# Taking the last output products of a group in one-pass forms, behind the group's last hidden block

## The chip, the cores and the metric

One core of one Trainium2 chip. The metric is the device time of one execution in microseconds (us). TensorE does matrix products into PSUM, ScalarE (ACT) and VectorE (DVE) do elementwise work and empty PSUM, SyncE's queue (SP) issues nearly all DMAs.

## The reference

Two blocks, one after the other. The first is a linear attention with RMS normalisation per head; the second a two-layer network with the activation h * erf(softplus(h)). All data are fp32 (the two weight matrices arrive as 64-bit floats).

```python
kv = np.einsum('bhsd,bhse->bhde', k, v)            # batch 8, heads 8, seq 576, head_dim 64
out = np.einsum('bhsd,bhde->bhse', q, kv)
rms = np.sqrt(np.mean(out * out, axis=-1, keepdims=True) + 1e-06)
out = out / rms * g_norm
x = out.transpose(0, 2, 1, 3).reshape(4608, 512)
h = x @ w_in                                       # w_in 512 x 2048
sp = np.maximum(h, 0.0) + np.log1p(np.exp(-np.abs(h)))
g = h * erf(sp)
out = g @ w_out                                    # w_out 2048 x 512
```

## The kernel before, in words

**Tiling.** The 4608 tokens are nine groups T of 512. Groups 0 to 7 are the first 512 tokens of each batch entry; the 64 left over from each entry make group 8. x is held transposed, as 4 blocks (one for each pair of heads, p = 0 to 3) of 128 features by 512 tokens. The 2048 hidden features are 16 blocks f of 128. One pair (T, f) is a *unit*. Its hidden product is 4 matmuls (h block = 128 features by 512 tokens), and its part of the output is 4 matmuls, one for each 128 tokens (column j), each adding 128 x 512 to a bank of PSUM.

**Two kinds of products.** A plain fp32 matmul is two instructions. In the other kind both factors are split into three forms (`upper`, `lower`: high, low, and both, a combination in which the low part is scaled by SHIFT = 4096). Products of high and low forms go to a bank n_ps, products of the third forms to a bank m_ps, and the result is n_ps * (SHIFT - 1) + m_ps. So three one-pass matmuls of type fp32r stand for one fp32 matmul. `product` (L581) writes such a group: eight matmuls into n_ps, then four into m_ps. The split of an operand is one ScalarE operation (high) and two VectorE operations (low, both).

**First stage, the loop at L893**, n = 0 to 32, n = T*16 + f, for groups 0 and 1. The weights lie in the chip's memory in fp32: `w_in_sb` and `w_out_sb`, one tile each, in the pool `first_w`. Group 0 and the first two units of group 1 use plain fp32. From f = 2 of group 1 on, hidden products are in forms (`hidden`, L634), with weights split on the way: `to_cut` says which weight block is split in which step, `w_upper` (L603) does the ScalarE part, `w_lower` (L619) the VectorE part one step later, and each split block is stored to DRAM for the later groups. A split goes into a buffer of the ring `w_in_p`, or, for the steps in `places_w`, into three slots of `w_in_sb` that are no longer needed (a *place*). Each unit is then: hidden product, n_ps emptied by ScalarE and m_ps added by VectorE (`add`, L567), softplus on ScalarE, later erf on ScalarE (a batch of four shares a table load), then the gate h * s on VectorE (`gates`, L886), and five steps (LAG) after the hidden product the four output products in plain fp32 (`project`, L644). In group 1 n_ps and m_ps take the same two banks (pool `ps_h`) in every unit. Units 28 to 31, the last four of group 1, don't go through `project`: their h block is kept (`old_h`) and their output products are taken in forms in the next stage. After unit 27's project the four sums are copied out of PSUM (`sums`, L673) by ScalarE and VectorE in turn.

**Attention in between.** The x of the next group is prepared during the loop, pair by pair, as pieces placed by `pieces_of` (L841): products (`visit`), the square's halves (`halve`), the mean (four small matmuls, then a table load, Ln, Exp, Square on ScalarE), `norm` (three VectorE operations, then a transpose for the next pair), `split` (one ScalarE and two VectorE operations into `x_forms`). For group 2 pair 3, the last, the mean comes at n = 30 and norm and split at n = 31.

**Second stage, from L1000.** Gates of units 28 to 31, then the pools of the first stage are closed, and the ring `w_out_p`, the tiles for `g_forms` and others are opened in that room. The loop at L1048 goes over batches m of four units: four hidden products in forms, then the output products of the batch before (`result`, L1023), with split weights loaded from DRAM (`load_parts`, L829). `load_parts("out", BATCH)` at L1046 issues the first four loads, for the output products of units 28 to 31, before the loop.

**Order.** Every engine works off its instructions in the order in which the program writes them (manual schedule); waits between engines are put in from the data that tiles share, reuse of a tile's room included.

Of the kernel before, what the change touches and what calls it, by code (L numbers as in the profile page):

```python
# [39 lines left out]
FP32 = mybir.dt.float32  # L40
# [10 lines left out]
BATCH = 4  # L51
# [18 lines left out]
def kernel(  # L70
# [106 lines left out]
    for i in range(NP):  # L177
        load_pair(i)

    w_in_sb = first_w.tile([P, FC, KC, P], FP32, name="w_in_sb")  # L180
    w_out_sb = first_w.tile([P, FC, DM], FP32, name="w_out_sb")


    g_col = const.tile([P, 1], FP32, name="g_col")
# [69 lines left out]
    def w_join(which, f, k):  # L254


        scaled, _, hi = words(which, f)
        e, m, late_ = w_cv.pop((which, f))
        w_raw.pop((which, f))
        if late_:  # L260
            nc.vector.tensor_scalar(
                out=e.bitcast(FP32), in0=scaled, scalar1=2.0**-112, scalar2=None, op0=ALU.mult
            )
        nc.vector.tensor_scalar(
            out=e, in0=e, scalar1=3, scalar2=None, op0=ALU.logical_shift_left
        )
        nc.vector.scalar_tensor_tensor(  # L267
            out=e, in0=hi, scalar=-(1 << 31), in1=e, op0=ALU.bitwise_and, op1=ALU.bitwise_or
        )
        if which == "in":  # L270
            out_ = w_in_sb[:, f : f + k].rearrange("p t c f -> p (t c f)")
        else:
            out_ = w_out_sb[:, f : f + k, :].rearrange("p t f -> p (t f)")
        nc.vector.tensor_tensor(out=out_.bitcast(I32), in0=e, in1=m, op=ALU.add)  # L274


# [269 lines left out]
    def thirds(x, high, low, both):  # L546
        upper(x, high)
        lower(x, high, low, both)

    def upper_w(x, high):  # L550
        nc.scalar.activation(high, x, AF.Copy, scale=(1.0 + 2.0**-13) / SHIFT)
# [46 lines left out]
                    )  # L598
        return n_ps, m_ps

    w_kept, w_new, w_now = {}, {}, {}

    def w_upper(which, f, place=None):  # L603


        if place is None:
            t = w_in_p.tile([P, 3, G], FP32R, name="w_new", tag="w")
            parts = t.rearrange("p i (c f) -> p i c f", c=KC)
        else:
            t = None  # L610
            parts = w_in_sb.bitcast(FP32R)[:, 3 * place : 3 * (place + 1)]
        if which == "in":
            x = w_in_sb[:, f]
        else:
            x = w_out_sb[:, f, :].rearrange("p (c f) -> p c f", c=KC)
        upper_w(x, parts[:, 0])
        w_new[which, f] = t, x, parts

    def w_lower(which, f):  # L619

        t, x, parts = w_new.pop((which, f))
        lower_w(x, *(parts[:, i] for i in range(3)))
        kept = w_kept[which, f] = dram.tile([P, 3, G], FP32, name=f"w_{which}{f}")
        for i in range(3):
            if t is None:
                nc.sync.dma_start(
                    out=kept[:, i].rearrange("p (c f) -> p c f", c=KC), in_=parts[:, i].bitcast(FP32)
                )
        if t is not None:
            nc.sync.dma_start(out=kept, in_=t.bitcast(FP32))  # L630
            if which == "in" and f >= WHOLE:
                w_now[which, f] = [t]
# [11 lines left out]
    def project(f, g, last):  # L644
        for j in range(J):
            if f == 0:
                o_ps[j] = ps_o.tile([P, DM], FP32, name=f"o_ps{j}", tag=f"o{j}")
            nc.tensor.matmul(  # L648
                o_ps[j],
                lhsT=g[:, j * P : j * P + P],  # L650
                rhs=w_out_sb[:, f, :],
                start=(f == 0),
                stop=last,
            )
# [186 lines left out]
    def pieces_of(T):  # L841


        steps = [([], [], [], []) for _ in range(FC)]
        for p in range(NP):
            products, apply, halve, mean, norm, split = attention(T, p)
            f = (BATCH - 1) * (p + 1) if T < FIRST else BATCH * p

            steps[f][2 if T == FIRST or p == 1 else 1].append(products)
            if T < FIRST and p == 0:  # L850
                steps[f + 2][3].append(apply)
            else:
                steps[f + 1][1].append(apply)
            steps[f + 2][3].append(halve)
            with_erf = (f + 2) % BATCH == BATCH - 1

            place = 2 if T < FIRST and p == 0 else 1
            steps[f + 2][place].append(partial(mean, table=not with_erf))
            steps[f + 3][0].append(norm)
            steps[min(f + 4, FC - 1)][0].append(split)  # L860
        return steps

    others = [("in", f) for f in range(WHOLE)]
    others += [("out", f) for f in (*range(FC - BATCH, FC), *range(FC - BATCH))]
    places_w = {3: 0, 5: 1, 6: 0, 8: 1, 9: 2, 10: 0}
    to_cut = {f: [] for f in range(FC)}
    for f in range(FC):
        if f < FC - BATCH:  # L870
            to_cut[f] = [others.pop(0), ("in", f + WHOLE)]
        elif f == FC - BATCH:
            to_cut[f] = [("in", FC - 2), ("in", FC - 1)]
        if f in places_w:
            to_cut[f].append((*others.pop(0), places_w[f]))
# [9 lines left out]

    def gates(n):  # L886
        nc.vector.tensor_tensor(out=hs[n], in0=hs[n], in1=ss[n], op=ALU.mult)  # L887

    def erf(units):
        for i in units:  # L890
# [2 lines left out]
    for n in range(FIRST * FC + 1):  # L893
# [37 lines left out]
        if T == FIRST - 1 and f >= WHOLE:  # L931
            n_ps, m_ps = hidden(T, f, turns=False)
        elif T < FIRST:

            if n >= AHEAD:
                plain[n] = ps_h.tile([P, G], FP32, name="h_ps", tag="h")
                blocks = [(n, c) for c in range(KC)]
            elif n == 0:
                for i, (pool, tag) in enumerate(((ps_now[0], "at"), (ps_now[0], "at"), (ps_o, "o0"))):
                    plain[i] = pool.tile([P, G], FP32, name="h_ps", tag=tag)  # L940
                blocks = [(i, c) for c in range(2) for i in range(2)]
                blocks += [(2, 0), (2, 1)] + [(i, 2) for i in range(3)] + [(0, KC - 1)]
            else:
                blocks = [(n, KC - 1)]
            for i, c in blocks:
                nc.tensor.matmul(  # L946
                    plain[i],
                    lhsT=w_in_sb[:, i % FC, c],
                    rhs=xT[T][:, c, :],
                    start=(c == 0),  # L950
                    stop=(c == KC - 1),
                )
        if T < FIRST:
            if n == whole:
                old_h = acc.tile([P, BATCH, G], FP32, name="h", tag="e")
            h = hs[n] = old_h[:, n - whole] if n >= whole else unit("h_sb")
            s = ss[n] = unit("s_sb")
            if n in plain:
                nc.scalar.copy(h, plain.pop(n))
            else:  # L960
                nc.scalar.activation(h, n_ps, AF.Copy, scale=SHIFT - 1.0)
                add(h, m_ps)
            if T == FIRST - 1:
                if f == 1:
                    x_both = wide.tile([P, KC, G], FP32R, name="x_both", tag="b")
                    for i in range(0, KC, 2):
                        both_only(x_high[:, i : i + 2], x_low[:, i : i + 2], x_both[:, i : i + 2])
                    x_forms[T] = x_high, x_low, x_both
                gates(done)
                for key in list(w_new):  # L970
                    w_lower(*key)
                for key in to_cut[f]:
                    w_upper(*key)
            if T == FIRST - 1 and f and f % BATCH == 0:
                erf(range(n - BATCH // 2, n))
                softplus_table()
            nc.scalar.activation(s, h, AF.Softplus)
            for piece in steps[f][1]:
                piece()
            if f % BATCH == BATCH - 1:  # L980
                apart = T == FIRST - 1 and f < FC - 1
                erf(range(n - BATCH + 1, n + 1 - (BATCH // 2 if apart else 0)))
                if not apart:
                    softplus_table()
            if T == FIRST - 1:
                load_parts("in", {FC - 3: 2, FC - 2: 1, FC - 1: 1}.get(f, 0))
        if n >= LAG:
            T2, f2 = divmod(n - LAG, FC)
            last = n - LAG in (FC - 1, whole - 1)
            project(f2, hs[n - LAG], last)  # L990
            if last:
                sums(*((acc, "e") if T2 < FIRST - 1 else (wide, "a")))
                if T2 == 0:
                    for j in range(J):
                        store(T2, j, es.pop(j))
        if T < FIRST:
            for piece in steps[f][2]:
                piece()
# [192 lines left out]
```

## Time and profile before

| | us |
|---|---|
| median of 3 runs | 907.13 |
| lowest, highest | 906.58, 907.44 |
| the profiled execution | 906.95 |
| its span, first to last instruction | 905.2 |

| engine | busy us | share of the span |
|---|---|---|
| PE (matmul) | 897.8 | 99% |
| VectorE | 758.9 | 84% |
| ScalarE | 593.0 | 66% |

The first stage ends at about 238 us of the span: the last output product of L648 begins in the last microseconds before that, and the first product of the second stage follows it. Times in microseconds below are from the span's start. PE, PEld, DVE, ACT and SPq in quoted lines are TensorE's matmuls, its weight loads, VectorE, ScalarE and SyncE's DMA queue; L648 is line 648 of the kernel.

### The profile page before, as it was taken

The page shows a single profiled execution, that of the slowest core. Times are in us where ns is not written, and L with a number is a line of the kernel's source. Part 1 is how long each engine was busy: PE and PEld are TensorE (multiplying, and loading weights), DVE is VectorE, ACT ScalarE, POOL GpSimd, SP SyncE. Part 2 cuts the span into 40 slices and gives each one's busy share as a digit, 9 for nine tenths or more (in the row PEclk, how much of TensorE's full clock was granted, in tenths as well). Part 3 has the DMA queues.
Part 4 walks back from the last instruction along what each step waited for, and adds up shares of the span by engine and source line. Part 5 has one row for each costly group of instructions (what it writes and reads, how often), then busy time and mean ns, then how long its engine had stood idle before and what let it go on. Part 6 is the DMA issues. An engine that isn't in the chain of part 4 may idle for free.

```text
span 905.2 us, 13406 instructions
## 1 busy us (share of the span) xinstructions
PE 897.8 (99%) x4938; PEld 668.6 (74%) x4938; DVE 758.9 (84%) x1093; ACT 593.0 (66%) x784; POOL 4.7 (1%) x14
## 2 busy tenths in 40 slices
PE   8999999999999999999999999999999999999998
PEld 4444446666688888888888888888888888888887
DVE  5799959997688888888888888888898888887677
ACT  5976667775766666666666666666666766665552
POOL 2000000000000000000000000000000000000000
PEclk9999999999999999999999999999999999999999
DMA  9967308999599988998899979988897788778871
GB/s 285 302 220 229 101 20 290 367 351 350 199 382 366 337 302 259 376 306 303 300 327 362 315 238 323 364 299 299 285 347 272 267 309 308 287 284 303 334 267 51
DMA packets 136929, 259.89 MB, mean 287 GB/s; under 512 B 78816, under 2 KB 87264, under 8 KB 136864
## 3 DMA queue, kind: packets, MB, share of 16 engines
q1 hardware_dynamic: 136128, 258.09, 81.3%
q10 hardware_dynamic: 544, 0.82, 0.3%
q8 instruction: 39, 0.64, 0.3%
q14 instruction: 26, 0.21, 0.1%
q0 software_dynamic: 192, 0.13, 0.0%
HBM read 224.40 MB, written 34.60 MB: 286 GB/s over the span
## 4 chain that ended last, share of the span: by engine, by line
PE 96%; ACT 2%; DVE 1%; issue 0%; DVEq 0%; ACTq 0%
PE n_ps L592 49%; PE m_ps L592 24%; PE o_ps L648 10%; PE h_ps L946 6%; PE at_ps L418 2%; PE at_ps L404 2%; PE at_ps L456 1%; PE at_ps L457 1%; PE warm_ps L795 1%; ACT w_m L251 0%; PE o_ps L715 0%; DVE w_in_sb L274 0%; DVE w_e L267 0%; PE ms_ps L722 0%; PE at_ps L412 0%
## 5 line engine op out<-in xcount | busy, mean ns | idle before, releaser
L592 PE MATMUL n_ps<-w_out_parts,g_forms 128*128 128x512 f32 (+1 forms) x936 | 230.9, 389 | 0.0
L592 PE MATMUL n_ps<-x_forms,w_in_parts 128*128 128x512 f32 x896 | 224.3, 392 | 0.0
L592 PEld LDWEIGHTS n_ps<-w_out_parts,g_forms 128*128 128x128 f32 x936 | 173.7, 188 | 35.5 <-DMA w_out_parts<-w_out 0.3
L592 PEld LDWEIGHTS n_ps<-x_forms,w_in_parts 128*128 128x128 f32 x896 | 166.6, 188 | 35.7 <-ACT s_sb L891 0.2
L567 DVE TENSOR_TENSOR h<-m_ps,h 128x512 f32<-128x512 f32 x116 | 78.2, 688 | 63.8 <-PE m_ps L592 61.8
L592 PE MATMUL m_ps<-w_out_parts,g_forms 128*128 128x512 f32 x464 | 124.0, 389 | 0.0
L592 PE MATMUL m_ps<-x_forms,w_in_parts 128*128 128x512 f32 x448 | 119.7, 389 | 0.0
L1097 ACT ACTIVATE h<-n_ps 128x512 f32<-128x512 f32 x112 | 66.2, 594 | 75.0 <-PE n_ps L592 74.7
L1102 ACT ACTIVATE s<-h 128x512 f32<-128x512 f32 x112 | 68.3, 628 | 70.1 <-DVE h L567 70.0
L648 PE MATMUL o_ps<-w_out_sb,h_sb 128*128 128x512 f32 x224 | 101.5, 596 | 0.2 <-DVE h_sb L887 0.2
L592 PEld LDWEIGHTS m_ps<-w_out_parts,g_forms 128*128 128x128 f32 x464 | 87.1, 188 | 18.5
L592 PEld LDWEIGHTS m_ps<-x_forms,w_in_parts 128*128 128x128 f32 x448 | 84.1, 188 | 17.5
L567 DVE TENSOR_TENSOR e<-m_ps,e 128x512 f32<-128x512 f32 x116 | 80.2, 692 | 15.2 <-PE m_ps L592 5.3
L648 PEld LDWEIGHTS o_ps<-w_out_sb,h_sb 128*128 128x128 f32 x224 | 41.3, 189 | 45.2 <-issue 43.1
L533 DVE SCALAR_TENSOR_TENSOR g_forms<-g_forms 128x1024 fp32r<-128x1024 f32 x58 | 71.1, 1225 | 2.0
L530 DVE TENSOR_TENSOR g_forms<-h,g_forms 128x1024 fp32r<-128x1024 f32 x58 | 70.6, 1217 | 1.1 <-ACT g_forms L527 1.1
L527 ACT ACTIVATE g_forms<-h 128x1024 fp32r<-128x1024 f32 x58 | 58.4, 1050 | 15.3 <-DVE h L1151 7.9
L562 DVE SCALAR_TENSOR_TENSOR e<-n_ps,e 128x512 f32<-128x512 f32 (+1 forms) x89 | 60.4, 678 | 7.2 <-PE n_ps L592 7.2
L946 PE MATMUL h_ps<-xT,w_in_sb 128*128 128x512 f32 x144 | 65.1, 595 | 1.2 <-DVE w_in_sb L274 1.1
L1151 DVE TENSOR_TENSOR h<-h,s 128x1024 f32<-128x1024 f32 x56 | 65.9, 1218 | 0.0
L116 ACT ACT_TABLE_LOAD x44 | 56.5, 1283 | 0.8
L946 PEld LDWEIGHTS h_ps<-xT,w_in_sb 128*128 128x128 f32 x144 | 26.9, 190 | 35.4 <-issue 31.4
(138 smaller groups left out, 1000.0 us busy)
## 6 DMA issues: line engine op xcount, KB each, us to landing
w_out_parts<-w_out SPq DMA_DIRECT2D x116, 768.0 KB, 7.1
w_in_parts<-w_in SPq DMA_DIRECT2D x112, 768.0 KB, 7.0
w_in<-w_new SPq DMA_DIRECT2D x16, 768.0 KB, 4.6
k_sb<-in_k_dram SPq DMA_DIRECT2D x32, 288.0 KB, 5.9
v_sb<-in_v_dram SPq DMA_DIRECT2D x31, 288.0 KB, 5.8
w_raw<-in_moe_w_in_dram SPq DMA_DIRECT2D x16, 512.0 KB, 5.5
w_raw<-in_moe_w_out_dram SPq DMA_DIRECT2D x8, 1024.0 KB, 4.9
out_dram<-e SPq DMA_DIRECT2D x32, 256.0 KB, 3.5
```

The lines of the kernel that those rows point to most:

```text
L116: nc.scalar.preload_act_table_set("softplus")
L527: nc.scalar.activation(high, x, AF.Copy, scale=1.0 + 2.0**-13)
L530: nc.vector.tensor_tensor(out=low, in0=x, in1=high.bitcast(FP32), op=ALU.subtract)
L533: nc.vector.scalar_tensor_tensor(out=both, in0=low.bitcast(FP32), scalar=SHIFT, in1=high.bitcast(FP32), op0=ALU.mult, op1=ALU.add,)
L562: nc.vector.scalar_tensor_tensor(out=out_, in0=ps, scalar=scale, in1=out_, op0=ALU.mult, op1=ALU.add)
L567: nc.vector.tensor_tensor(out=out_, in0=ps, in1=out_, op=ALU.add)
L592: nc.tensor.matmul(ps[:, cols], lhsT=weights(form, k), rhs=moving(form, k)[:, cols], start=(form == forms[0] and k == 0), stop=(form == fo ...
L648: nc.tensor.matmul(o_ps[j], lhsT=g[:, j * P : j * P + P], rhs=w_out_sb[:, f, :], start=(f == 0), stop=last,)
L946: nc.tensor.matmul(plain[i], lhsT=w_in_sb[:, i % FC, c], rhs=xT[T][:, c, :], start=(c == 0), stop=(c == KC - 1),)
L1097: nc.scalar.activation(h[:, i], n_ps, AF.Copy, scale=SHIFT - 1.0)
L1102: nc.scalar.activation(s[:, i], h[:, i], AF.Softplus)
L1151: nc.vector.tensor_tensor(out=part(h, half), in0=part(h, half), in1=part(s, half), op=ALU.mult)
```

## The change

The output products of units 24 to 27 (blocks 8 to 11 of group 1) no longer go through `project`.

- The splits of output weights 8 to 11 stay on the chip (`w_held`): 8 and 10 were already split into places of the input-weight room, 9 and 11 now are too (place 3 and place 1). The stores to DRAM remain. For this the two weight tiles become eight pair tiles each (two blocks in a tile).
- The gates of units 26 and 27 come at n = 29, behind the gate of unit 25. `hold` splits g of unit 24 at n = 29, of 25 and 26 at n = 30, of 27 at n = 31, behind that step's softplus, into pair tiles of the output-weight room.
- At n = 32 `held_sums` takes the products of the four units in forms, sixteen for each column: those of the third forms into the bank of `o_ps`, the others into n_ps. Columns 0 and 1 first, units in the order in which they are ready; columns 2 and 3 follow when the two n_ps banks are free again. ScalarE copies n_ps out with the factor, VectorE adds `o_ps`.
- Mean, norm and split of group 2's last pair move from n = 30 and 31 into `held_sums`, and the erfs of units 28 to 31 from n = 31 to between its columns. One table load falls away, as no softplus follows that mean.

```diff
+    def pair_tile(which, i, kind, name):
+        return first_w.tile([P, 2, G], kind, name=name, tag=f"{which}{i}")
+    w_in_sb = [pair_tile("in", i, FP32, "w_in_sb") for i in range(FC // 2)]
+    w_out_sb = [pair_tile("out", i, FP32, "w_out_sb") for i in range(FC // 2)]
...
-            parts = w_in_sb.bitcast(FP32R)[:, 3 * place : 3 * (place + 1)]
+            slots = range(3 * place, 3 * (place + 1))
+            for i in sorted({slot // 2 for slot in slots} - set(w_places)):
+                w_places[i] = pair_tile("in", i, FP32R, "w_place")
+            parts = [one(w_places, slot) for slot in slots]
+            if FC - 2 * BATCH <= f < FC - BATCH:
+                w_held[f] = parts
...
             place = 2 if T < FIRST and p == 0 else 1
+            if T == FIRST and p == NP - 1:
+                ending.extend((partial(mean, table=False), norm, split))
+                continue
...
+    held_w = {FC - 7: 3, FC - 5: 1}
...
-            to_cut[f] = [others.pop(0), ("in", f + WHOLE)]
+            other = others.pop(0)
+            if other[0] == "out" and other[1] in held_w:
+                other = (*other, held_w[other[1]])
+            to_cut[f] = [other, ("in", f + WHOLE)]
...
+    def hold(n):
+        i = 2 * (n - whole + BATCH)
+        tiles = [pair_tile("out", i + k, FP32R, "g_held") for k in range(2)]
+        forms = g_held[n] = tiles[0][:, 0], tiles[0][:, 1], tiles[1][:, 0]
+        thirds(hs[n], *forms)
+    def held(ps, n, j, forms, start, stop):
+        for form in forms:
+            nc.tensor.matmul(
+                ps,
+                lhsT=g_held[n][form][:, j * P : j * P + P],
+                rhs=w_held[n % FC][form],
+                start=start and form == forms[0],
+                stop=stop and form == forms[-1],
+            )
+    def both_held(n):
+        for j in range(J):
+            held(o_ps[j], n, j, (2,), False, n == whole - 1)
+    def held_sums():
+        mean, norm, split = ending
+        mean()
+        units = range(whole - BATCH, whole)
+        n_ps = [None] * J
+        all_e = wide.tile([P, J, DM], FP32, name="e", tag="a")
+        es.update((j, all_e[:, j]) for j in range(J))
+        for j in range(2):
+            n_ps[j] = ps_h.tile([P, G], FP32, name="n_ps", tag="h")
+        for group in (units[:2], units[2:3], units[3:]):
+            for n in group:
+                both_held(n)
+            for j in range(2):
+                for n in group:
+                    held(n_ps[j], n, j, (0, 1), n == units[0], n == units[-1])
+        norm()
+        split()
+        for j in range(J):
+            if j >= 2:
+                n_ps[j] = ps_h.tile([P, G], FP32, name="n_ps", tag="h")
+                for n in units:
+                    held(n_ps[j], n, j, (0, 1), n == units[0], n == units[-1])
+            if j >= 2:
+                erf(range(whole + 2 * j - 4, whole + 2 * j - 2))
+            nc.scalar.activation(es[j], n_ps[j], AF.Copy, scale=SHIFT - 1.0)
+            add(es[j], o_ps[j])
+        softplus_table()
...
-                gates(done)
+                if done < whole - 2:
+                    gates(done)
                 for key in list(w_new):
                     w_lower(*key)
                 for key in to_cut[f]:
                     w_upper(*key)
+                if n == whole + 1:
+                    gates(whole - 2)
+                    gates(whole - 1)
...
+            for i in {whole + 1: (0,), whole + 2: (1, 2), whole + 3: (3,)}.get(n, ()):
+                hold(whole - BATCH + i)
-            if f % BATCH == BATCH - 1:
+            if f % BATCH == BATCH - 1 and n < whole:
                 apart = T == FIRST - 1 and f < FC - 1
                 erf(range(n - BATCH + 1, n + 1 - (BATCH // 2 if apart else 0)))
...
-        if n >= LAG:
+        if LAG <= n < whole - BATCH + LAG:
...
+        if n == FIRST * FC:
+            held_sums()
```

More of the change, by code (lines that the diff above doesn't have):

```diff
@@ L178, with one, blocks_of @@
         load_pair(i)
-    w_in_sb = first_w.tile([P, FC, KC, P], FP32, name="w_in_sb")
-    w_out_sb = first_w.tile([P, FC, DM], FP32, name="w_out_sb")
+    def pair_tile(which, i, kind, name):
+        return first_w.tile([P, 2, G], kind, name=name, tag=f"{which}{i}")
+    w_in_sb = [pair_tile("in", i, FP32, "w_in_sb") for i in range(FC // 2)]
+    w_out_sb = [pair_tile("out", i, FP32, "w_out_sb") for i in range(FC // 2)]
+    def one(tiles, f):
+        return tiles[f // 2][:, f % 2]
+    def blocks_of(x):
+        return x.rearrange("p (c f) -> p c f", c=KC)
     g_col = const.tile([P, 1], FP32, name="g_col")
@@ L269, in w_join @@
         )
[L270 to L273, printed above, removed]
+        out_ = (w_in_sb if which == "in" else w_out_sb)[f // 2][:, f % 2 : f % 2 + k]
+        out_ = out_.rearrange("p t f -> p (t f)")
         nc.vector.tensor_tensor(out=out_.bitcast(I32), in0=e, in1=m, op=ALU.add)
@@ L599, in product @@
         return n_ps, m_ps
-    w_kept, w_new, w_now = {}, {}, {}
+    w_kept, w_new, w_now, w_held, w_places = {}, {}, {}, {}, {}
     def w_upper(which, f, place=None):
@@ L607, in w_upper @@
             t = w_in_p.tile([P, 3, G], FP32R, name="w_new", tag="w")
-            parts = t.rearrange("p i (c f) -> p i c f", c=KC)
+            parts = [t[:, i] for i in range(3)]
         else:
             t = None
-            parts = w_in_sb.bitcast(FP32R)[:, 3 * place : 3 * (place + 1)]
[L612 to L616, printed above, removed]
+            slots = range(3 * place, 3 * (place + 1))
[4 more added lines that the diff above has]
+                w_held[f] = parts
+        x = one(w_in_sb if which == "in" else w_out_sb, f)
+        upper_w(x, parts[0])
         w_new[which, f] = t, x, parts
@@ L621, in w_lower @@
         t, x, parts = w_new.pop((which, f))
-        lower_w(x, *(parts[:, i] for i in range(3)))
+        lower_w(x, *parts)
         kept = w_kept[which, f] = dram.tile([P, 3, G], FP32, name=f"w_{which}{f}")
@@ L625, in w_lower @@
             if t is None:
-                nc.sync.dma_start(
-                    out=kept[:, i].rearrange("p (c f) -> p c f", c=KC), in_=parts[:, i].bitcast(FP32)
-                )
+                nc.sync.dma_start(out=kept[:, i], in_=parts[i].bitcast(FP32))
         if t is not None:
@@ L650, in project @@
                 lhsT=g[:, j * P : j * P + P],
-                rhs=w_out_sb[:, f, :],
+                rhs=one(w_out_sb, f),
                 start=(f == 0),
@@ L861, in pieces_of @@
         return steps
+    ending = []
     others = [("in", f) for f in range(WHOLE)]
@@ L887, in gates @@
         nc.vector.tensor_tensor(out=hs[n], in0=hs[n], in1=ss[n], op=ALU.mult)
+    g_held = {}
+    def hold(n):
[42 more added lines that the diff above has]
+        softplus_table()
     def erf(units):
@@ L947 @@
                     plain[i],
-                    lhsT=w_in_sb[:, i % FC, c],
+                    lhsT=blocks_of(one(w_in_sb, i % FC))[:, c],
                     rhs=xT[T][:, c, :],
@@ L986 @@
                 load_parts("in", {FC - 3: 2, FC - 2: 1, FC - 1: 1}.get(f, 0))
-        if n >= LAG:
+        if LAG <= n < whole - BATCH + LAG:
             T2, f2 = divmod(n - LAG, FC)
-            last = n - LAG in (FC - 1, whole - 1)
+            last = n - LAG == FC - 1
             project(f2, hs[n - LAG], last)
             if last:
[L992 to L995, printed above, removed]
+                sums(acc, "e")
+                for j in range(J):
+                    store(T2, j, es.pop(j))
+        if n == FIRST * FC:
+            held_sums()
         if T < FIRST:
```

## Prediction

> **What bounds the kernel now.** I read the page's engine shares first, then the chain of waits in the stretch that the change touches (205 to 262 us), then that stretch's timelines engine by engine, then the DMA queue's own waits. In what follows n is the unit counter of the first loop; unit n is the hidden block n % 16 of group n // 16, so the change concerns units 24 to 27.
>
> ```profile
> PE 897.8 (99%) x4938; PEld 668.6 (74%) x4938; DVE 758.9 (84%) x1093; ACT 593.0 (66%) x784; POOL 4.7 (1%) x14
> L648 PE MATMUL o_ps<-w_out_sb,h_sb 128*128 128x512 f32 x224 | 101.5, 596 | 0.2 <-DVE h_sb L887 0.2
> ```
>
> TensorE works all the time, and a microsecond taken from its stream is worth a microsecond only if nothing else steps into the gap. The 224 matmuls of L648 are 112 fp32 products, two instructions each. Their real pace is not the 596 ns of a record (records overlap) but the spacing, which the chain view gives (start, length, what):
>
> ```profile
> 210.49 3.44 PE o_ps L648 x8
> 213.92 1.87 PE n_ps L592 x8
> 215.79 0.94 PE m_ps L592 x4
> ...
> 248.17 1.81 PE n_ps L592 x8
> 249.99 0.91 PE m_ps L592 x4
> ```
>
> One unit's four output products take 3.44 us; twelve one-pass matmuls of L592 take 2.72 us (1.81 + 0.91), 0.227 us each. The next view is the end of the second group on ScalarE and VectorE (start, length, engine, line, operation, idle before it):
>
> ```profile
> 225.87 1.28 ACT L113 ACT_TABLE_LOAD   x1
> 231.45 0.63 ACT L527 ACTIVATE x_forms<-x 128x512 fp32r<-128x512 f32 x1 [0.97 <-DVE x L488]
> 236.11 2.19 ACT L891 ACTIVATE s_sb<-s_sb 128x512 f32<-128x512 f32 x4
> 233.45 0.68 DVE L567 TENSOR_TENSOR h<-m_ps,h 128x512 f32<-128x512 f32 x1
> 238.28 2.49 DVE L887 TENSOR_TENSOR h<-h,s_sb 128x512 f32<-128x512 f32 x4
> ```
>
> From the table load of the last mean to the finished x is 5.6 us in which each step waits for the one before. The four gates of units 28 to 31 end at 240.77. What hangs on them is in the DMA queue's waits (total, times, longest), the queue's timeline and the weight-load timeline:
>
> ```profile
> SPq L837 <- DVE h L887: 8.3, 1, 8.3
> 240.83 2.14 SPq L837 DMA_DIRECT2D w_out_parts<-w_out  x4
> 252.14 0.30 PEld L592 LDWEIGHTS n_ps<-w_out_parts,g_forms 128*128 128x128 f32 x2 [0.31 <-DMA w_out_parts<-w_out]
> ```
>
> The reader is to see one tight link: the first four output-weight loads lie in the room of the first stage, they start 0.06 us after the last gate, and TensorE waits for the fourth of them at 252.14, 11.3 us later. So the end of gates(31) already sets when the first output products of the next stage can run. After 262 us TensorE is busy in every microsecond until the last window, so what is lost by then is lost for good.
>
> **What the Trainium skill says.** "FP8 and Floating Point Precision", TensorE Precision Notes, has true fp32 as four passes through the array; the trace agrees roughly: 3.44 us for four products is 0.86 each against 0.227, a ratio of 3.8. "TensorE: Matmul & The Clock Gate", Architectural detail, says ScalarE and VectorE queues are strict FIFO; the trace agrees: add(31) at 233.45 stood 2.5 us behind the norm and split, though its products were done at about 230.9. The same page, HAM oscillation, warns of idle gaps above about 3.4 us, after which the array runs at half clock. Before, the granted clock is 1.00 in every window and no gap here exceeds about 1 us, so no run shows this yet. "ScalarE: Activation LUTs", What ACT_TABLE_LOAD costs, gives 1283 ns; the trace has 1283.
>
> **The change, part by part.** *TensorE.* Removed: 4 units x 3.44 = 13.76 us. Added: 4 units x 4 columns x 3 forms = 48 one-pass matmuls x 0.227 = 10.88 us. Sum -2.88. Also the stall before project(27) goes (project(26) at 230.96 + 3.44 = 234.40, next start 234.79): -0.4. Alone these would give -3.3.
>
> *Weights kept.* Units 9 and 11 get split places in the input-weight room instead of ring buffers. Same ScalarE and VectorE work (0.52 and 1.33 us of queue time per split, as before). Their stores become three DMAs each, four more issues of about 0.35 us on SP at n = 27 to 29. SP already sits there waiting for VectorE (issue groups of 4.10 and 5.51 us for three stores), so I take zero; without that cover it would be 1.4 us on SP, before loads nobody waits for until 238. The output weights of units 8 to 11 also leave pair tiles whose reuse needs earlier readers done; by the timeline those are done (project(23) ends 213.9). Zero.
>
> *Splits of g and their place.* Four hold() steps: ScalarE 0.52 us each, VectorE 0.72 + 0.61 = 1.33 us each (spacing of such pairs at 213.44 to 214.77). Gates 26 and 27 move forward to n = 29, 0.61 each. These stand in FIFO order ahead of things that matter. I step through it with the durations of the trace:
>
> n = 29: add(29) 216.83 and gates(25) 217.44 stay; gates 26, 27 free VectorE at 218.7; split 24 (upper on ScalarE by 219.2) ends at 220.6. n = 30: the halve and tail steps, 2.21 us before (218.71 to 220.92), now run 220.6 to 222.8, and add(30) stands behind them: 222.8 to 223.5. TensorE, with no project between, does hidden(30) from 218.0 to 220.8, but the m_ps part of hidden(31) needs the bank that add(30) reads: ready at 222.6, started at 223.5, a new stall of 0.9; done 224.4. softplus(30) at 223.5, then the uppers of 25 and 26; VectorE splits them from 224.7 to 227.4, and add(31) stands behind: 227.4 to 228.1. softplus(31), the upper of 27, and only then (229.15) the mean's table load, which before came at 225.87: 3.3 later. norm makes x 5.6 us after, at 234.7.
>
> *held_sums.* TensorE: mean 0.5 from 224.4; units 24 and 25 with about 0.4 of waits (split 25 done 226.1, the second bank free with add(31) at 228.1); unit 27's split is done at 230.7; columns 0 and 1 end about 232.7. Column 2 needs the bank of column 0, emptied by a ScalarE copy, and that copy is queued behind split's upper, which waits for x at 234.7. So upper 234.7 to 235.25, copy 0 done 235.85, and TensorE idles 3.2 us. Columns 2 and 3 (16 x 0.227 = 3.6) end at 239.6 to 239.7, where before hidden(2,0) began at 238.49: **+1.2 us** instead of -3.3.
>
> ScalarE goes on: copy 1 to 236.3, erf table to 237.6, two erfs (0.54 each) to 238.65, copy 2 to 239.2, two erfs to 240.3, copy 3 done 240.8. VectorE: add of column 3 to 241.5, the four gates 2.49, end **243.9**, 3.2 later than 240.77. One erf-side table load less (softplus after the mean) is already in this.
>
> *Who waits for the gates.* The four w_out_parts loads start at 244.0 instead of 240.83, the fourth is in at 244.0 + 11.3 = 255.3. TensorE arrives there at 251.83 + 1.2 = 253.0 and waits 2.3 us instead of 0.3. Net: **+3.2 us**. Bounds of this last term: 0 if those loads no longer bind (they come in 2 us sooner), and the full 3.2 as taken; a later input load competing could add about 1 us. I take 11.3 again, since SP's order is unchanged: the k, v, q and input-weight loads of the next group are queued behind these four and move with them. The bank stall has bounds 0 (copy served before the split) and 3.9 (chain 0.7 later); I take 3.2 from the order written.
>
> Sum against the profiled execution: 906.95 (span 905.2) + 3.2 = 910.15; the median of the three runs is 907.13, 0.18 above it. Forecast **910.2**.
>
> **Rivals.** (1) *TensorE's sum decides*: the ScalarE/VectorE chain is covered, no stalls, 906.95 - 3.3 = 903.7. For it: 99% busy TensorE. Against: it needs column 0's copy done by 232.7, thus x 3.2 us sooner, and gates(31) by about 237.5; it decides from there. Chance 0.13. (2) *The loads do not bind*: they wait for the room's readers alone or land faster; only the +1.2 stays, 908.3. Against: the wait for L887 is the one the queue shows. Chance 0.17. (3) *The clock drops* in the 3.2 us gap: 16 products at half pace, +3.6 on copies, gates and loads, 913.6. The gap is just below the page's 3.4, estimate only. Chance 0.10. The forecast's own band, 909.0 to 911.5, has 0.60.
>
> **How the numbers follow.** About 0.2%, 1.8 us, is what a measurement of this kernel can tell from no change, so "same" is 905.3 to 908.9. Faster 0.13 (rival 1), same 0.17 (rival 2), slower 0.70 (forecast and rival 3). The range 907.0 to 913.0 holds the forecast, rival 2 and about half of rival 3's spread; left out are rival 1 and the top.
>
> **What would show it.** Right: a gap on TensorE of about 3 us in held_sums, released by a ScalarE copy of n_ps; mean's table load near 229; gates ending near 244; w_out_parts issued right after; LDWEIGHTS of the first result waiting about 2 us for DMA. A DMA wait under 0.5 us there, or gates that end by 241, would prove the load step wrong; a gap under 1 us in held_sums the bank step; a granted clock below 1.0 would be rival 3.

## The result and the profile after

The changed kernel takes 910.66 us (median of 6 runs, 909.1 to 912.1), the kernel before 907.1 (6 runs, 906.2 to 907.4): ratio 1.0041, 95% interval 1.0028 to 1.0054. It is slower by 3.6 us; the forecast was 910.2. The profiled execution took 910.55, with a span of 908.8. Of the 3.6 us between the two spans 0.36 already stand at the first output product (46.54 against 46.18 us), long before the changed place; so profile times after are compared with times before plus 0.36.

From the page of the kernel after, the engine shares and the group of fp32 output products (now line 656, 32 matmuls fewer):

```profile
PE 897.4 (99%) x4954; PEld 673.0 (74%) x4954; DVE 765.1 (84%) x1103; ACT 594.7 (65%) x789; POOL 4.7 (1%) x14
L656 PE MATMUL o_ps<-w_out_sb,h_sb 128*128 128x512 f32 x192 | 87.0, 596 | 0.0
```

The shares hardly show that anything went wrong: TensorE is "99% busy" as before. The chain of waits shows it (start, length, what):

```profile
227.62 0.70 DVE h L575
228.34 0.63 ACT s_sb L1050
228.97 0.52 ACT g_held L535
229.50 1.28 ACT L113
...
234.30 0.76 DVE x L496
...
235.09 0.63 ACT x_forms L535
235.72 0.49 ACT e L954
...
236.25 5.26 PE n_ps L917 x16
```

It runs over ScalarE and VectorE: softplus of unit 31, the split of g of unit 27, the mean's table load, x, its split, and only then the copy (L954) that frees a bank for the products of column 2. Before the change the chain ran over these engines too, but only up to the gate of unit 27, and from there over TensorE without a break:

```profile
234.13 0.61 DVE h_sb L887
...
234.79 3.70 PE o_ps L648 x8
238.49 1.83 PE n_ps L592 x8
```

There TensorE had stood still for 0.2 us. Now it has a hole, a stretch in which it does nothing:

```profile
232.14 1.07 PE L917 MATMUL n_ps<-w_place,g_held 128*128 128x512 f32 x4
236.25 0.79 PE L917 MATMUL n_ps<-w_place,g_held 128*128 128x512 f32 x1 [3.04 <-ACT e L954]
```

Four one-pass matmuls from 232.14 are through at about 233.05, so the hole is 3.2 us (the record's ends are modelled, hence its 3.04). What follows it is as telling. In the table of windows the column behind the busy times is the granted clock:

```profile
235.00:236.00 1.00, 0.00 (x0) 0.00 (x0) 0.96 (x3) 0.91 (x2) 0.00 (x0) 0.85 0.00 0
236.00:237.00 1.00, 0.74 (x2) 0.65 (x3) 0.97 (x2) 0.98 (x3) 0.00 (x0) 0.50 0.00 0
...
238.00:239.00 1.00, 1.00 (x4) 0.71 (x4) 0.37 (x1) 1.00 (x2) 0.00 (x0) 0.50 0.00 0
239.00:240.00 1.00, 1.00 (x6) 0.83 (x5) 0.00 (x0) 0.45 (x2) 0.00 (x0) 0.95 0.00 0
```

From about 235.7 to 239.1, 3.4 us, TensorE is granted half its clock (0.85 over the window from 235 to 236 is half clock for its last 0.3 us, 0.95 over that from 239 for its first 0.1). Columns 2 and 3 take 5.26 us instead of some 3.8. The six timed runs differ in the same way: mean clock 1.000 at 909.1 us, 0.998 in four runs from 910.5 to 911.0, 0.995 at 912.1; 3.4 us at half clock take 0.002 off the mean. The last link, on VectorE, the DMA queue and the weight loads:

```profile
242.78 2.48 DVE L904 TENSOR_TENSOR h<-h,s_sb 128x512 f32<-128x512 f32 x4
```

```profile
245.41 2.03 SPq L845 DMA_DIRECT2D w_out_parts<-w_out  x4
```

```profile
255.43 0.30 PEld L600 LDWEIGHTS n_ps<-w_out_parts,g_forms 128*128 128x128 f32 x2 [0.56 <-DMA w_out_parts<-w_out]
```

As before, the four loads start with the last gate (245.26) and TensorE waits for the fourth. It is ready at 255.43, 3.29 us later than the 252.14 of before. That is the loss: 0.36 of start-up, 2.9 of the changed place, and 0.3 in the rest.

### The profile page after: what moved, and what is told of

It reads as the page before. It is cut to its first block, busy times and chain, and to the rows that moved or that the text cites. A ratio compares the mean times of both kernels' runs of the same rounds, so it can differ in the third digit from the quotient of the medians.

```text
span 908.8 us, 13463 instructions
## 1 busy us (share of the span) xinstructions
PE 897.4 (99%) x4954; PEld 673.0 (74%) x4954; DVE 765.1 (84%) x1103; ACT 594.7 (65%) x789; POOL 4.7 (1%) x14
## 4 chain that ended last, share of the span: by engine, by line
PE 92%; DVE 3%; DMA 2%; ACT 2%; SPq 0%; issue 0%; DVEq 0%
PE n_ps L600 48%; PE m_ps L600 24%; PE o_ps L656 9%; PE h_ps L1015 6%; PE at_ps L426 2%; PE at_ps L412 2%; DMA w_out_parts<-w_out 1%; DMA q_sb<-in_q_dram 1%; PE at_ps L465 1%; PE at_ps L464 1%; PE n_ps L917 1%; DMA w_raw<-in_moe_w_out_dram 1%; DVE w_in_sb L282 0%; DVE h L904 0%; DVE w_e L277 0%
## 5 line engine op out<-in xcount | busy, mean ns | idle before, releaser
L656 PE MATMUL o_ps<-w_out_sb,h_sb 128*128 128x512 f32 x192 | 87.0, 596 | 0.0
L656 PEld LDWEIGHTS o_ps<-w_out_sb,h_sb 128*128 128x128 f32 x192 | 35.6, 190 | 38.2 <-issue 37.3
```

The source lines that it names most:

```text
L656: nc.tensor.matmul(o_ps[j], lhsT=g[:, j * P : j * P + P], rhs=one(w_out_sb, f), start=(f == 0), stop=last,)
```

## Experiments

Theory A, after the result: three links in a row make the loss. The copies of columns 0 and 1 stand in ScalarE's queue behind a split that waits for x (the hole); the hole halves the clock (1.4 us more); the gates, and with them the loads, come late. Rivals: B, the splits of g make the hole; C, only the end of the gates counts. Times are medians; "before" was run beside each (906.8 to 907.1).

**Copies first.** One edit in `held_sums`:

```diff
+        for j in range(2):
+            nc.scalar.activation(es[j], n_ps[j], AF.Copy, scale=SHIFT - 1.0)
         norm()
         split()
...
             if j >= 2:
                 erf(range(whole + 2 * j - 4, whole + 2 * j - 2))
-            nc.scalar.activation(es[j], n_ps[j], AF.Copy, scale=SHIFT - 1.0)
+                nc.scalar.activation(es[j], n_ps[j], AF.Copy, scale=SHIFT - 1.0)
             add(es[j], o_ps[j])
```

> The two ScalarE copies that free the banks of columns 0 and 1 are queued ahead of the last pair's norm and split; nothing else moves. Theory A (the 3.0 us gap on TensorE comes from these copies standing behind the split's upper in ScalarE's queue, and the half clock after it comes from the gap): the gap shrinks to under 0.8 us, the granted clock stays 1.00, the sixteen products of columns 2 and 3 take 3.7 us instead of 5.3, the gates end near 243.4 and the time falls by about 2 to 908.7. Theory B (the late splits of g on VectorE make the gap): the gap stays above 2.5 us and the time at 910.7.

Measured: 908.5 (ratio to before 1.0018, 1.0009 to 1.0026). TensorE's timeline:

```profile
233.38 3.92 PE L917 MATMUL n_ps<-w_place,g_held 128*128 128x512 f32 x16 [0.23 <-ACT e L946]
238.65 2.11 PE L600 MATMUL n_ps<-x_forms,w_in_parts 128*128 128x512 f32 x8 [1.36 <-ACT e L956]
```

The hole is down to 0.2 us, the products take 3.92, no window shows a clock under 1.00; the gates end at 243.26. B falls. What is left shows in the second line: the next stage's first product now waits 1.36 us for the copy of column 2, and the fourth load costs 1.25 us (before: 0.31).

**Fill the hole, keep the waits.** Twelve matmuls by zero go into the output banks; a tile of zeros is made at the start of the kernel, and the mark for the last product of each output bank moves to these matmuls.

```diff
...
+        for k in range(12):
+            nc.tensor.matmul(
+                o_ps[k % J], lhsT=zero, rhs=w_held[FC - BATCH - 1][0], start=False, stop=(k >= 8)
+            )
         norm()
         split()
```

> Twelve one-pass matmuls with an all-zero stationary operand, 2.7 us, are put into the gap; they add zeros to the output sums. All waits of the changed kernel stay. Theory A (idleness halves the clock): the clock stays 1.00, the sixteen products that follow take 3.7 us instead of 5.3, the gates end about 1.4 us earlier, and the time falls by about 1.2 to 909.5; the six timed runs lie closer together. Theory B (the clock falls for another cause, or the half clock is hidden behind the loads): clock still below 1.00 on average, or time unchanged at 910.7.

Measured: 909.09 (1.0027, 1.0016 to 1.0039), six runs from 908.6 to 910.1.

```profile
232.85 2.88 PE L948 MATMUL o_ps<-w_place,zero 128*128 128x512 f32 x12
236.10 3.92 PE L919 MATMUL n_ps<-w_place,g_held 128*128 128x512 f32 x16 [0.37 <-ACT e L960]
```

Column 2 starts no sooner (236.10; 236.25 without the fill), but at full clock: its sixteen products and those of column 3 take 3.92, and no run of the six has a mean clock under 0.999. Useless work saves 1.6 us. So idleness halves the clock, and that is on the path. The loads now wait 0.99 us: part of what the clock gives back the loads take.

**Gates early, gates late.** In one kernel the four erfs and gates stand ahead of columns 2 and 3, in another four extra multiplications on dead data stand ahead of the gates (the erfs and gates that the first kernel moves are taken out of their old places):

```diff
         for j in range(J):
+            if j == 2:
+                erf(range(whole, whole + BATCH))
+                for n in range(whole, FIRST * FC):
+                    gates(n)
...
```

```diff
+    for turn_ in range(4):
+        dead = whole - 3 + turn_ % 3
+        nc.vector.tensor_tensor(out=ss[dead], in0=ss[dead], in1=ss[dead], op=ALU.mult)
     for n in range(whole, FIRST * FC):
         gates(n)
```

> The four erfs and the four gates are put ahead of the copies and sums of columns 2 and 3. The gap and the order before it stay. Theory A (gap and half clock are on the path, the loads only fill what is left, 0.6 us of wait): gates end near 241, loads are issued 4 us sooner, the DMA wait at the first result goes, TensorE arrives no sooner, time falls by 0.6 to about 910.1. Theory C (the end of the gates alone sets the time through the loads, as the prediction's last term had it): the time falls by 2 us or more, to 908.5 or below.

> Four extra VectorE multiplications on data no longer used, 2.5 us, stand ahead of the four gates. Theory A and C (the loads of the first output weights start with the last gate and bind): loads issued 2.5 us later, the DMA wait at the first result grows by 2.5 us, time about 913.2. Rival (the loads have slack, the wait of 0.6 us is by chance): time rises by under 0.8, to at most 911.5.

Gates early: 910.26 (1.0041, 1.0029 to 1.0053).

```profile
235.38 5.54 PE L917 MATMUL n_ps<-w_place,g_held 128*128 128x512 f32 x16 [3.08 <-ACT e L956]
```

```profile
240.95 2.14 SPq L845 DMA_DIRECT2D w_out_parts<-w_out  x4
```

The loads are issued at 240.95, the DMA wait is gone, the hole and the half clock stay. C falls: with the loads 4.5 us sooner only about 0.4 comes back, less than the runs of either kernel differ among themselves. Gates late: 915.42 (1.0080, 1.0062 to 1.0098), more than the 913.2 expected. The direction is as expected and the size was missed, for a reason that the windows show:

```profile
236.00:242.00 6.00, 6.00 (x14) 4.67 (x15) 2.65 (x5) 4.38 (x7) 0.00 (x0) 0.50 0.00 0
256.00:259.00 3.00, 0.80 (x3) 0.30 (x2) 2.50 (x4) 1.80 (x4) 0.00 (x0) 1.00 0.99 406
259.00:263.00 4.00, 3.92 (x12) 3.28 (x13) 2.91 (x4) 3.97 (x4) 0.00 (x0) 0.57 1.05 370
```

The longer DMA wait (3.4 us in three pieces by the records of the weight loads, from 255 to 259) is itself a hole and halves the clock once more, and the first half-clock stretch lasts 6.8 us here, twice as long. Two of the six runs had a mean clock of 1.000: 911.0 and 911.6, 1.9 and 2.5 above the changed kernel's one run at that clock. That is the rise that was expected, without what the clock adds. So the loads have no slack: sooner, they bring almost nothing; later, they cost about as much as they are late.

**The same delay in the kernel before.** The four multiplications ahead of its gates.

> The kernel before the change, with four extra VectorE multiplications on data no longer used, 2.5 us, ahead of the four gates. Theory A (already there the loads of the first output weights start with the last gate and land just in time): time rises by 2.2 to 2.6, to about 909.4. Rival (the wait of 0.3 us at that load was by chance, the loads have slack of microseconds): rise under 0.8, at most 907.8.

Measured: 912.38 (1.0062, 1.0049 to 1.0074), more than twice the rise expected. The weight loads:

```profile
251.77 0.30 PEld L592 LDWEIGHTS n_ps<-w_out_parts,g_forms 128*128 128x128 f32 x2 [0.87 <-DMA w_out_parts<-w_out]
253.62 0.30 PEld L592 LDWEIGHTS n_ps<-w_out_parts,g_forms 128*128 128x128 f32 x2 [1.55 <-DMA w_out_parts<-w_out]
255.47 0.50 PEld L592 LDWEIGHTS n_ps<-w_out_parts,g_forms 128*128 128x128 f32 x2 [1.56 <-DMA w_out_parts<-w_out]
```

The prediction's reading holds: in the kernel before these loads have no slack. The wait is 4.0 us instead of 0.3 (2.35 us of later issue, and 12.3 us from issue to the fourth landing instead of 11.3), and the clock halves in its last piece, from about 254.4 to 261.2 (windows of 2 us have 0.61, 0.50, 0.50 and 0.69 from 254 to 262).

**One part undone.** Mean, norm and split back at n = 30 and 31 (the `ending` lines removed). With them comes back the table load of 1.28 us that had fallen away.

> One part of the change undone: mean, norm and split of the last pair stay at n = 30 and 31, as in the kernel before, with the rest of the change in place. Theory A (what stands ahead in ScalarE's queue sets TensorE's waits): the mean's table load and three functions now stand ahead of the splits of g of units 25 and 26; the gap moves forward to the products of unit 25 and grows to over 4 us, the clock halves there too, and the time rises to about 913.5. Rival (the moved mean, norm and split are what costs): the time falls to 908 or below.

Measured: 916.83 (1.0108, 1.0093 to 1.0124). Direction as expected, 3.3 us more than expected. TensorE's timeline:

```profile
223.05 0.36 PE L464 MATMUL at_ps<-sq_hi,mean_w 128*128 128x256 f32 x1 [1.97 <-DVE bd_kv L362]
...
230.93 1.21 PE L914 MATMUL o_ps<-w_place,g_held 128*128 128x512 f32 x4 [1.92 <-DVE g_held L541]
235.52 3.78 PE L914 MATMUL n_ps<-w_place,g_held 128*128 128x512 f32 x8 [3.38 <-ACT h L1023]
```

I had priced the wait for the split of unit 25 alone. The mean's matmuls, just ahead of hidden(31), now wait 2.0 us for VectorE, and the clock is at half from about 223.6 to 227.0, right after this hole; and, worst, the ScalarE operation that empties n_ps of unit 31 stands behind the split of x: the same fault as in `held_sums`, at another bank. So moving mean, norm and split was not what costs; with the products so late they cost more where they were.

**Towards a better version.** Each adds an edit: copies first together with gates early (the adds of columns 0 and 1 go ahead of x's split); then the first products of the second stage take the banks in another order; then the halving of the last pair's square comes behind add(30).

```diff
     load_parts("out", BATCH)
+    banks[:4] = banks[2:4] + banks[:2]
```

```diff
-            for piece in steps[f][3]:
-                piece()
+            if n != whole + 2:
+                for piece in steps[f][3]:
+                    piece()
...
+                if n == whole + 2:
+                    for piece in steps[f][3]:
+                        piece()
```

> Copies of columns 0 and 1 ahead of norm and split, as in the first experiment, and the four erfs and gates ahead of columns 2 and 3. Theory A (each wait is set by what stands ahead in ScalarE's queue): the gates end near 240 and the DMA wait of 1.25 us at the first result goes, but the copy of column 2, now behind four erfs, frees the bank of the next stage's first product only at 239.8 instead of 238.6: one wait for the other, time 908.5 as with the copies alone. Theory C (the loads alone decide): 907.2 or below.

> As the kernel before it in this list, and the first product of the second stage takes the banks of output columns 0 and 1, which are empty earlier, instead of the two n_ps banks. Theory A: no bank wait at the start of the second stage (first product near 237.4), no DMA wait, granted clock 1.00; against the version with the copies alone 2.6 us less, 905.9, about 1 us under the kernel before the change. Rival (another wait comes in, by x of the last pair or by the loads): 907 or more.

> As the version with the banks exchanged, and the halving of the last pair's square stands behind the add of unit 30 on VectorE instead of ahead of it. Theory A: the 1.0 us for which the third forms of unit 31 wait goes, splits of g and all behind them come about 1 us sooner: 905.0. Rival (the chain over ScalarE is as long, the wait only moves to held_sums): 905.9, as without it.

Measured 908.85 (1.0023, 1.0014 to 1.0032), 906.68 (0.9996, 0.9987 to 1.0004) and 905.89 (0.9991, 0.9983 to 1.0000). The first trades one wait for the other, as expected: the loads' wait goes, and

```profile
238.79 2.11 PE L600 MATMUL n_ps<-x_forms,w_in_parts 128*128 128x512 f32 x8 [2.39 <-ACT e L958]
```

its ten runs fall in two groups, five at a clock of 0.999 or 1.000 (907.6 to 908.5) and five at 0.997 or 0.998 (909.2 to 910.3). With the banks exchanged that hole is gone (first product at 236.49), but the loads are late again: 2.4 us of wait, which I had expected to be nil, because the fourth took 12.2 us from the first issue instead of about 10. (The profiled execution, 907.4, is one of the slower of its 13.) So 0.8 of the 2.6 us expected against the copies alone is missing. The halving behind the add takes out the wait for the third forms of unit 31 and brings 0.8 of the 0.9 expected of it; a DMA wait of 1.3 us is left. Neither version can be told from the kernel before: both intervals reach 1.

**Freeing the loads from the gates.** Twice, on top of the last version: the erfs of units 28 to 31 write to another tile, first the one of x's dead low form, then the one of x's dead third form. And the first of these in the kernel before.

```diff
-        erf(range(whole, whole + BATCH))
+        s_low = low.tile([P, BATCH, G], FP32, name="s_low", tag="x_low")
+        for i in range(BATCH):
+            nc.scalar.activation(s_low[:, i], ss[whole + i], AF.Erf)
...
+            ss[whole + i] = s_low[:, i]
```

```diff
-        s_low = low.tile([P, BATCH, G], FP32, name="s_low", tag="x_low")
+        s_low = wide.tile([P, BATCH, G], FP32, name="s_low", tag="b")
```

> As the version with the halving behind the add, and the erfs of units 28 to 31 are written into another tile (the one of the dead low form of x), so that the gates no longer read the room into which the first output weights are loaded. Theory A (the loads wait for the gates only because the gates read that room): the four loads are issued about 2 us sooner, near 237.5, right after the last erf; the DMA wait of 1.3 us at the first result goes; 1.0 to 1.3 less than that version, 904.7. Rival (the loads land no sooner, or the wait is for something else in that room): 905.9 as before.

> The kernel before the change, with the erfs of units 28 to 31 written into the other tile in the same way, and nothing else. Theory A: its loads no longer wait for the gates but for the last output products of unit 27 (about 238.3 instead of 240.8); only the DMA wait of 0.3 us can go: 906.8, no change that can be measured. Rival (loads 2.5 us sooner save more, as other waits hang on them): 906.0 or less.

> As the attempt to free the loads from the gates, but the erfs of units 28 to 31 are written into the room of the dead third form of x, which stays open all through and in which no output weight is ever loaded. Theory A (the loads wait for the gates because these read room that the loads use; the tile of the earlier attempt lay at the edge of that room): now the four loads are issued right after the last erf, near 238.5, 1.5 to 2 us sooner; the DMA wait of 1.3 us goes; 904.9. Rival (the loads wait for the last gate whatever it reads): loads near 240, wait 1.3, time 905.9 to 906.5.

The first failed: 906.47 (0.9991, 0.9983 to 0.9999). In its queue the loads still start with the last gate (which ended at 240.11), and the DMA wait is 1.4 us:

```profile
240.18 2.17 SPq L845 DMA_DIRECT2D w_out_parts<-w_out  x4
```

The same tile in the kernel before: 906.98 (1.0001, 0.9993 to 1.0009), loads at 240.75, likewise right after the gates; so it says nothing on what freed loads would bring there. The second tile works: 904.79 (0.9974, 0.9964 to 0.9984). Queue waits, queue and TensorE:

```profile
SPq L845 <- ACT s_low L953: 1.8, 1, 1.8
```

```profile
237.33 2.11 SPq L845 DMA_DIRECT2D w_out_parts<-w_out  x4
```

```profile
247.75 1.98 PE L600 MATMUL n_ps<-w_out_parts,g_forms 128*128 128x512 f32 x8
249.56 1.07 PE L600 MATMUL m_ps<-w_out_parts,g_forms 128*128 128x512 f32 x4
```

The loads go with the last erf, 1.5 us ahead of the end of the last gate (238.84), and the first output products run through without a wait. So it is the room that the gates read or write that ties the loads, as theory A says; that the low form's tile belongs to this room, since its pool is closed at the same place, is my inference from the contrast of the two. This version is faster than both kernels: 2.3 us under the one before, 5.9 under the change.

## Why the prediction was right, and where not

**The mechanism.** Right in the hole and in the time (910.2 against 910.66), wrong in how the time comes about. The 2.9 us of TensorE work and the 0.4 us stall do go, and what takes their place is first of all the queue order that the prediction wrote down. But of its 3.2 us the prediction put 1.2 on TensorE being late at the end of the first stage and 2.0 on the wait for the loads. The profile has 2.7 (241.51 less 0.36 against 238.49) and 0.25 (0.56 against 0.31).

**Step by step**, measured times less 0.36. Third forms of unit 31 wait 0.9: measured about 0.8. The mean's table load at 229.15: 229.14. x at 234.7: 234.7. The hole 3.2: 3.2. Up to there the chain of durations from the trace of before, laid out in the new order, was right to a tenth.

**Columns 2 and 3 in 3.6 us: wrong**, 5.26. This was rival 3, given a chance of 0.10 and a price of 3.6; the clock did drop, for 3.4 us in the profile and by the mean clock in five of six runs, at about 1.4 us. The first stage ended at 241.15 instead of 239.7. The prediction set the 3.2 us hole against the 3.4 of the Trainium skill ("TensorE: Matmul & The Clock Gate", HAM oscillation) and gave the drop little chance; the runs disagree with that reading: the clock falls after shorter holes (below).

**Gates at 243.9**: 244.9, the clock's doing.

**Loads 11.3 us to the fourth landing: too long**, 10.0 here. With TensorE itself later, the wait at the first result was 0.56 instead of 2.3, hardly above the 0.5 under which the prediction would have called its load step wrong. The link is there, as the late gates show, but it adds little in this kernel, as the early gates show.

The two errors cancel: about 1.4 too little for the clock, about 1.3 too much for the loads. Without the drop the time is 909.1 (the one run at clock 1.000; with the zero fill the median is 909.1 too), 2.0 over before; with the prediction's chain and the loads as measured, 243.9 + 10.0 against 252.1 of before, it would be 1.8. So the right number is partly luck; the right sign is not: at full clock too the change loses, by the hole and the late gates.

**Rival 1** (TensorE's sum decides, 903.7) named the right conditions: copies not behind x, gates sooner. The last version, with further edits, comes near to them (its gates end at 238.84; 237.5 was asked for) and to 904.8. **Rival 2** (loads don't bind, or land faster) is half right: they do land faster, but they bind, as the delayed gates show in both kernels.

**Two sums.** 235.85 + 3.6 is 239.5, not 239.6 to 239.7, and rival 3's 910.15 + 3.6 is 913.8, not 913.6. Neither changes the argument.

What stays open: why the fourth load needs 10.0 to 10.1 us after the first issue in some profiles (the changed kernel, copies first, zero fill, gates late, mean back) and 11.3 to 12.3 in others (before, the bank exchange, delayed gates in the kernel before). The loads asked for are the same, in the same order. What the DMA records show is that in the first set 3.5 MB had moved when the fourth was in, at some 350 GB/s, and in the kernel before 4.0 MB at 356: there more of the later loads had gone along with the four, and 0.5 MB at this rate are about 1.4 us (an estimate from these numbers). In the kernel before with late gates the rate was lower too, 307 GB/s. Why the shares differ is not shown.

## What to carry to other kernels

Where the matmul engine is full, a saving in its stream is worth only what the emptying engines' queue order lets through: before moving work behind a group, list for each bank which instruction frees it and what stands ahead of that instruction, in order, and put bank-freeing copies ahead of anything that waits for a long chain. In this program a load into reused room starts with the last reader of that room; if the loads are tight, move that reader's operand elsewhere. And to a hole of two microseconds or more on TensorE add the price of half clock, here about 1.6 us for one stretch, times its chance: half the runs at 2.4 us, most at 3.

## What the runs showed of the hardware

- Half clock after a hole. Only one run of each kernel has a profile, so the counts below are runs with a mean clock under 0.999, and that the hole is as long in a kernel's other runs is assumed. Holes of 3.0 to 3.2 us: 14 of 17 runs (5 of 6 of the change, 5 of 5 with gates early, 4 of 6 with gates late, which has a second hole). Of 2.4 us (copies and gates): 5 of 10. Of 1.4 us or less (copies first): none of 11; and of the three versions with DMA waits of up to 1.5 us at the first result (bank exchange, halving late, the first attempt to free the loads) 1 of 39, a run of 908.6 where the others of its kernel took 905.4 to 906.4.
- There is no sharp limit between these. With the mean back, half clock followed a hole of 2.0 us by the record, while three runs with holes of 3.0 to 3.2 us kept the full clock.
- One stretch of half clock costs about 1.6 us: the two groups of runs of copies and gates differ by that (means 908.2 and 909.8), and the zero fill saves as much.
- The half clock lasts about 3.4 us in the changed kernel's profile and 6.8 us, twice that, in both kernels with late gates.
- Three short waits in a row with a little work between (4.0 us by the records of the weight loads, 0.45, 1.12 and 1.12 us by those of the matmuls, within 5 us, the kernel before with late gates) halve the clock too, in all five runs by the mean clock.
- Twelve matmuls by zero in the hole, which change nothing in the sums, keep the clock up and make the changed kernel 1.6 us faster (909.09 against 910.66).
